# Gated attention and an MLP mixer on one core: the second channel product as seven block products in place of eight

## The chip, the cores and the metric

The kernel runs on one core of a Trainium2 chip. A core has five engines with a queue each, worked off in order: TensorE (PE, matmuls; its weight loads are listed apart as PEld), VectorE (DVE), ScalarE (ACT), GpSimd (POOL) and SyncE (SP, which here issues transfers). Sixteen DMA engines move data between the chip's memory (DRAM) and the core's on-chip memory, SBUF, and transpose blocks on the way. Matmul results land in PSUM. The metric is the time of one execution in microseconds (us), as a median of several runs.

## The reference

Inputs are `u`, `v` (8 batches × 3008 rows × 256), `z` (8 × 3008 × 64) and four mixer weights. All is float32; the kernel multiplies in bfloat16 and sums in float32.

```python
scores = (1.0 / S) * np.matmul(z, z.transpose(0, 2, 1))      # S = 3008
attn = np.maximum(scores, 0.0) ** 2
x = u * np.matmul(attn, v)

h = np.maximum(x.transpose(0, 2, 1) @ w_tok1, 0.0) @ w_tok2  # over the rows, 3008 -> 256 -> 3008
u1 = x + h.transpose(0, 2, 1)
h2 = np.maximum(u1 @ w_ch1, 0.0)                             # 256 -> 1536
out = u1 + h2 @ w_ch2                                        # 1536 -> 256
```

The last line's `h2 @ w_ch2` is the "second channel product", `u1 @ w_ch1` the first. They are called ch2 and ch1 below.

## The kernel before

**Tiles.** Rows are worked in query blocks of 512 (QW), six a batch (NQ), the last 448 wide; 448 is three tiles of 128 rows (P) and a half tile of 64, and the half tiles of an even batch and the next odd one are multiplied together ("hs", "ut"). The 1536 channels are 12 tiles of 128 (CHT).

**Stages.** For a batch, attention runs block by block: scores (L428), relu on ACT (L466), square on DVE (L474), the product with `v` (L657). The score matrix is symmetric, so a computed block also serves mirrored, by a DMA transpose on SP into a tile of the pool "fl" ("flip"). The copy and the add of the accumulators (L783, L789) and the gate with `u` (L810) give `x` with its columns on the partitions (pool "xT"); one more DMA transpose gives its rows (`turn_x`, pool "x"). Mixer: token product 1 (`tok1`, L864), token product 2 (`tok2`, L883) with its add into xT (L892), then for each query block six pieces of ch1 and up to four of ch2. Blocks 3 to 5 of one batch are mixed together with the token products and blocks 0 to 2 of the next, in one stretch of TensorE work of some 70 us before that batch's successor begins its attention. Seven such stretches follow a first short one.

**A piece of ch1** (`ch1`, L913): two channel tiles, eight matmuls at most 512 columns wide into a pair of PSUM banks (hp, L924), then one relu of the whole pair into a tile of the pool "h2", on ACT (L967) or on DVE (L969), whichever is expected to be free earlier (L960). **A piece of ch2** (`ch2`, L978): for one tile of 128 rows twelve matmuls, each with 128×128 of h2 as the loaded weights and 256 columns of `w_ch2` as the moving side (L993). Two pieces fill a bank; then one DVE add (L1009, or L1027 for the odd ends) puts `u1` to it in a buffer "res" (three of them), and SP sends this to the output (L1014, L1030). The rows of `u1` come by a DMA transpose on SP (`turn_u2`, L906, pool "us").

**The order.** It is fixed when the program is built. A planner goes through time with assumed costs: `Piece` is a piece of TensorE work with its needs, `push` puts work on ACT, DVE or SP, `run_engines` lets those queues come up to a time, `next_piece` (L1083) takes the next mixer piece out of two lists, `heads` (token products) and `tails` (ch1 and ch2). A piece that `opens` a PSUM pair is one of a chain until the one that `closes` it, and only one such chain is open at a time. `ROOM` (L316) limits the buffers of each pool that the plan has in use. PSUM has a ring of bank pairs. What the planner does not count still holds: the instructions wait, by semaphores, for the tiles, banks and buffers that they use. The tails of a batch are listed thus, with `early` being 2:

```python
        for q in range(NQ):
            for c2 in range(early if q else 0, CHT // 2):
                add_ch1(q, c2, q)
            if q + 1 < NQ:
                for c2 in range(early):
                    add_ch1(q + 1, c2, q)
            for half in halves(q):
                for i in range(pieces_of(q, half)):
                    add_ch2(q, half, i)
```

So all four pieces of ch2 of a block stand together, behind two pieces of ch1 of the next block.

Of the kernel before, what the change touches and what calls it, by code (L numbers as in the profile page):

```python
# [45 lines left out]
class Piece:  # L46


    def __init__(self, cost, needs, fn, opens=False, closes=False, room=None,
                 urgent=False, key=(0, 0)):  # L50
        self.cost, self.needs, self.fn = cost, needs, fn
        self.opens, self.closes, self.room = opens, closes, room
        self.urgent, self.key = urgent, key
# [3 lines left out]
def kernel(  # L57
# [42 lines left out]
    w_ch2_sb = consts.tile([P, CHT, D], BF16)  # L100
    ident = consts.tile([P, P], BF16)
# [53 lines left out]
    def first_z(c):  # L155

        zf = sb.tile([P, GK, d_qk], F32, tag="x", name="zf", bufs=7)
# [9 lines left out]
    def double_first_z(c):  # L167
        zr = sb.tile([P, GK, 2, d_qk], BF16, tag="h2", name="zr0", bufs=8)
        nc.vector.tensor_copy(zr[:], zf0[c].unsqueeze(2).to_broadcast([P, GK, 2, d_qk]))  # L169
        return zr  # L170
# [28 lines left out]
    def load_v(b, c):  # L199
# [5 lines left out]
        else:  # L205
            vt = sb.tile([P, GK, D], BF16, tag="v", name="v_sb", bufs=8)
# [108 lines left out]
    live = {"at": 0, "fl": 0, "xT": 0, "x": 0, "h2": 0, "us": 0}  # L315
    ROOM = {"at": 6, "fl": 10, "xT": 9, "x": 7, "h2": 8, "us": 2}  # L316
# [155 lines left out]
    def square(unit, view, t):  # L472
# [15 lines left out]
        if flips(b, q, g):  # L488
# [4 lines left out]
                        room=lambda: has_room(("fl",)) and (  # L493
# [21 lines left out]
    def flip_tiles(a3, j):  # L515
# [4 lines left out]
        return a3  # L520

# [93 lines left out]
    def do_whole(start, g):  # L615
# [19 lines left out]
        if final:  # L635
# [3 lines left out]
                room=("xT", "x") if dh == 0 else lambda: (blk.b, blk.q) in xTs)  # L639
# [127 lines left out]
    def finish(blk, dh, end):  # L767
# [12 lines left out]
        def copy(t):  # L780
            cp = sb.tile([P, QW], F32, tag="res", name="cp", bufs=3)
# [6 lines left out]
        def add(cp, t):  # L788
            nc.vector.tensor_add(cp[:, :W], acc[:, 0, :W], cp[:, :W])  # L789
            push("dve", t, 0.58, 0.7, lambda t: gate(blk, dh, cp, t), first=1,  # L790
                 room=(lambda: (blk.b, blk.q) in uTs and has_room(("xT", "x"))) if dh == 0
# [7 lines left out]
    def gate(blk, dh, acc, t):  # L799
        b, q, W = blk.b, blk.q, blk.W  # L800
        uT = uTs[b, q]
        if dh == 0:
            xTs[b, q] = sb.tile([P, DT, QW], BF16, tag="xT", name="xT", bufs=ROOM["xT"])
            live["xT"] += 1
            live["x"] += 1
# [11 lines left out]
        if dh == DT - 1:  # L817
            gated[0] += 1
            push("sp", t, 1.25, 7.5 if q < NQ - 1 else 12.0, lambda t: turn_x(b, q, t), first=1,
                 room=lambda: b == 0 or mode[0] == "full")  # L820

    def turn_x(b, q, t):
        x = sb.tile([P, DT, QW // P, P], BF16, tag="x", name="x_sb", bufs=ROOM["x"])
# [14 lines left out]
    before = [None]  # L838

# [7 lines left out]
    def add_mixer(b):  # L847
# [3 lines left out]
        h2_done = {}  # L851
# [60 lines left out]
        def ch1(q, c2, end):  # L912
# [3 lines left out]
            if c2 == 0:  # L916
                live["us"] += 1
                st["turned", q] = push("sp", u_done[q].t, 1.25, 5.5, lambda t: turn_u2(q))
            live["h2"] += 1
# [8 lines left out]
            def load(e):  # L928
                return max(free[e], end) + sum(op.busy for op in waiting[e])

# [7 lines left out]
            if (b, q, c2) == (B - 1, NQ - 1, CHT // 2 - 1):  # L938
                landed, freed = [], Done()

                def evacuate_part(r, t):
                    if not landed:
                        st["h2", q, c2] = sb.tile(
                            [P, 2, QW], BF16, tag="h2", name="h2pre", bufs=ROOM["h2"])
                    h2 = st["h2", q, c2]
# [14 lines left out]
            on_act = load("act") + 0.92 < load("dve") + 1.15  # L960

            def evacuate(t):
                h2 = sb.tile([P, 2, QW], BF16, tag="h2", name="h2pre", bufs=ROOM["h2"])
                st["h2", q, c2] = h2
# [5 lines left out]
                if q == NQ - 1:  # L970
                    keep_ends(h2)
            engine, busy = ("act", 0.92) if on_act else ("dve", 1.15)
            ring.append((push(engine, end + 0.21, busy, busy + 0.16, evacuate,
                              done=h2_done[q, c2]), slot))
            if c2 == CHT // 2 - 1:
                release("xT", xT_uses[q])

        def ch2(q, half, i, end):  # L978
# [9 lines left out]
            for cc in range(CHT):  # L988
                if both:
                    h2 = pair["hs"][:, cc, :]  # L990
                else:
                    h2 = st["h2", q, cc // 2][:, cc % 2, c0:c0 + P]
# [3 lines left out]
            over = i == pieces_of(q, half) - 1 and half == halves(q)[1]  # L996
            if over:
                live["h2"] -= CHT // 2
# [3 lines left out]
            def residual(t):  # L1002
                us = st["u", q]
                if q == NQ - 1 and b % 2 == 0 and half == 0:
                    pair["ut"] = sb.tile([TAIL, DT, P], BF16, tag="ut", name="ut", bufs=1)
                    nc.gpsimd.tensor_copy(pair["ut"][:], us[:TAIL, :, full_tiles[q], :])
                res = sb.tile([P, 2, D], F32, tag="res", name="res", bufs=3)
# [9 lines left out]
                else:  # L1017
                    k = half * 2
                    j = i if apart else 0
                    ends = [(j, slice(0, P), us[:, :, k + j, :],  # L1020
                             rows_of(out[b], q)[:, k + j, :])]
# [10 lines left out]
                if over:  # L1032
                    live["us"] -= 1
# [9 lines left out]
        def add_ch1(q, c2, by):  # L1043
            h2_done[q, c2] = Done()
            tails.append(Piece(4 * column_time(widths[q]), [u_done[q]] + w_done[:2],
                               lambda end: ch1(q, c2, end),
                               room=("h2", "us") if c2 == 0 else ("h2",),
                               key=(b, 2 + by)))

# [8 lines left out]
        def alone(q, half):  # L1058

            return pieces_of(q, half) == 1 or (b, q, half) == (B - 1, NQ - 1, 0)  # L1060

        def add_ch2(q, half, i):
            two = not alone(q, half)
            needs = [Sooner(h2_done[q, c2], 0.218 * c2) for c2 in range(CHT // 2)]
            tails.append(Piece(1.312, needs + w_done[2:],
                               lambda end: ch2(q, half, i, end), opens=two and i == 0,
                               closes=two and i == 1, key=(b, 2 + q)))


        early = ROOM["h2"] - CHT // 2  # L1070
        for q in range(NQ):
            for c2 in range(early if q else 0, CHT // 2):
                add_ch1(q, c2, q)
            if q + 1 < NQ:
                for c2 in range(early):
                    add_ch1(q + 1, c2, q)
            for half in halves(q):
                for i in range(pieces_of(q, half)):
                    add_ch2(q, half, i)
# [3 lines left out]
    def next_piece(t):  # L1083
# [3 lines left out]
        if opened[0] is not None:  # L1087
# [374 lines left out]
```

## Time and profile before

| what | value |
|---|---|
| runs, median (lowest to highest) | 1142.33 us (1141.83 to 1142.89) |
| span of the profiled execution | 1140.2 us |
| ch2 matmuls (L993) | 2208, 273 ns each as recorded |
| ch1 matmuls (L924) | 1152, 375 ns each |
| product with `v` (L657) | 2738 + 1680, 374 and 367 ns each |
| relu of ch1 on ACT (L967) / DVE (L969) | 159 of 998 ns / 128 of 1215 ns |
| granted TensorE clock | 9 tenths or more in all 40 slices |

The span is the profiler's, from the first to the last instruction; it is 2.1 us below the median of the runs. A recorded matmul lasts longer than the step from one to the next, since matmuls are pipelined; how long a stretch of them takes is read from the chain of waits or from the timeline. The idle time of an engine is given with its releaser, the instruction that ended it.

### The profile page before, as it was taken

The page shows a single profiled execution, that of the slowest core. Times are in us where ns is not written, and L with a number is a line of the kernel's source. Part 1 is how long each engine was busy: PE and PEld are TensorE (multiplying, and loading weights), DVE is VectorE, ACT ScalarE, POOL GpSimd, SP SyncE. Part 2 cuts the span into 40 slices and gives each one's busy share as a digit, 9 for nine tenths or more (in the row PEclk, how much of TensorE's full clock was granted, in tenths as well). Part 3 has the DMA queues.
Part 4 walks back from the last instruction along what each step waited for, and adds up shares of the span by engine and source line. Part 5 has one row for each costly group of instructions (what it writes and reads, how often), then busy time and mean ns, then how long its engine had stood idle before and what let it go on. Part 6 is the DMA issues. An engine that isn't in the chain of part 4 may idle for free.

```text
span 1140.2 us, 22490 instructions
## 1 busy us (share of the span) xinstructions
PE 1133.2 (99%) x9219; PEld 678.5 (60%) x9219; DVE 642.1 (56%) x953; ACT 549.3 (48%) x702; POOL 146.3 (13%) x387
## 2 busy tenths in 40 slices
PE   9999999999999999999999999999999999999998
PEld 3455464665557655576555765556655576556666
DVE  6887744464654556645565455654566544644543
ACT  7998635234752346522574236632366322732231
POOL 4500110221002110021101211012100120000000
PEclk9999999999999999999999999999999999999999
DMA  9999953987959878697986968679598794782122
GB/s 165 186 171 213 164 126 80 173 164 130 170 119 195 154 136 161 116 199 141 161 147 118 211 139 154 136 132 209 116 168 146 144 197 103 142 139 72 51 84 65
DMA packets 469928, 165.25 MB, mean 145 GB/s; under 512 B 433665, under 2 KB 447553, under 8 KB 469825
## 3 DMA queue, kind: packets, MB, share of 16 engines
q1 hardware_dynamic: 441968, 131.11, 56.7%
q0 software_dynamic: 27344, 32.32, 20.5%
q8 instruction: 72, 1.18, 0.4%
q10 hardware_dynamic: 512, 0.38, 0.1%
q14 instruction: 32, 0.25, 0.1%
HBM read 65.40 MB, written 24.64 MB: 79 GB/s over the span
## 4 chain that ended last, share of the span: by engine, by line
PE 98%; DMA 1%; DVE 0%; ACT 0%; issue 0%
PE acc L657 41%; PE op L993 22%; PE hp L924 21%; PE sc L428 6%; PE a_ps L864 4%; PE h_ps L883 3%; PE first_acc L573 1%; DMA zT<-zr 1%; DMA zf<-in_z_dram 0%; DVE zr L169 0%; ACT h2pre L967 0%; DVE h2pre L949 0%; ACT h2pre L947 0%; PE up L1257 0%; DVE res L1027 0%
## 5 line engine op out<-in xcount | busy, mean ns | idle before, releaser
L657 PEld LDWEIGHTS <-v_sb 64*128 64x128 bf16 x4418 | 241.9, 94 | 215.8 <-issue 1.8
L657 PE MATMUL acc<-at,v_sb 64*128 64x512 bf16 (+1 forms) x2738 | 338.8, 374 | 0.0
L466 ACT ACTIVATE at<-sc 128x1024 bf16<-128x1024 f32 (+1 forms) x290 | 286.2, 1026 | 73.4 <-PE sc L428 63.3
L967 ACT ACTIVATE h2pre<-hp 128x1024 bf16<-128x1024 f32 (+1 forms) x159 | 158.8, 998 | 310.8 <-PE hp L924 310.8
L474 DVE TENSOR_TENSOR at<-at 128x1024 bf16<-128x1024 bf16 (+1 forms) x290 | 197.5, 687 | 125.0 <-ACT at L466 120.9
L924 PE MATMUL hp<-xT,w_ch_sb 128*128 128x512 bf16 (+1 forms) x1152 | 255.3, 375 | 0.1
L993 PE MATMUL op<-w_ch_sb,h2pre 128*128 128x256 bf16 x2208 | 251.3, 273 | 0.1
L993 PEld LDWEIGHTS <-h2pre 128*128 128x128 bf16 x2208 | 216.0, 98 | 36.3 <-ACT h2pre L947 0.4
L969 DVE TENSOR_SCALAR h2pre<-hp 128x1024 bf16<-128x1024 f32 (+1 forms) x128 | 155.5, 1215 | 80.9 <-PE hp L924 80.9
L657 PE MATMUL acc<-fl,v_sb 64*128 64x512 bf16 (+1 forms) x1680 | 190.7, 367 | 0.0
L924 PEld LDWEIGHTS <-w_ch_sb 128*128 128x128 bf16 x1152 | 112.2, 98 | 126.7 <-issue 3.0
L1009 DVE TENSOR_TENSOR res<-op,u_sb 128x512 f32<-128x512 f32 x87 | 60.2, 691 | 174.9 <-PE op L993 170.9
L428 PE MATMUL sc<-zT 64*128 64x512 bf16 (+1 forms) x732 | 132.4, 359 | 0.6 <-DMA zT<-zr 0.5
L454 ACT ACTIVATE at<-sc 128x512 bf16<-128x512 f32 (+3 forms) x152 | 56.5, 442 | 84.0 <-PE sc L428 73.5
L789 DVE TENSOR_TENSOR cp<-acc,cp 128x512 f32<-128x512 f32 (+1 forms) x94 | 63.5, 675 | 38.2 <-ACT cp L783 37.8
L783 ACT COPY cp<-acc 128x512 f32<-128x512 f32 (+1 forms) x89 | 51.8, 582 | 54.8 <-PE acc L657 54.7
L506 DVE TENSOR_TENSOR at<-at 128x512 bf16<-128x512 bf16 (+3 forms) x152 | 42.1, 321 | 47.5 <-ACT at L454 47.5
L428 PEld LDWEIGHTS <-zT 64*128 64x128 bf16 x732 | 42.6, 94 | 43.4 <-issue 3.5
L810 DVE TENSOR_TENSOR xT<-cp,uT 128x512 bf16<-128x512 f32 (+1 forms) x94 | 62.4, 664 | 1.5
L892 DVE TENSOR_TENSOR xT<-xT,h_ps 128x1024 bf16<-128x1024 bf16 (+1 forms) x48 | 56.1, 1175 | 12.5 <-PE h_ps L883 12.4
L121 POOL CAST mark<-at 128x1 f32<-128x1 bf16 x12 | 2.3, 188 | 414.5 <-DVE at L474 414.5
L883 PE MATMUL h_ps<-w_tok_sb,a_sb 128*128 128x512 bf16 (+1 forms) x192 | 47.9, 375 | 0.0
(59 smaller groups left out, 315.0 us busy)
## 6 DMA issues: line engine op xcount, KB each, us to landing
out_dram<-res SPq DMA_DIRECT2D x87, 256.0 KB, 2.5
v_sb<-in_v_dram POOLq DMA_DIRECT2D x40, 256.0 KB, 5.7
ur<-in_u_dram POOLq DMA_DIRECT2D x40, 256.0 KB, 4.7
w_tok_sb<-in_moe_w_tok_dram POOLq DMA_DIRECT2D x10, 256.0 KB, 9.5
zs<-in_z_dram POOLq DMA_DIRECT2D x35, 64.0 KB, 2.8
at<-at SPq DMA_TRANSPOSE x114, 2.3
fl<-at SPq DMA_TRANSPOSE x105, 5.3
v_sb<-in_v_dram POOLq DMA_DIRECT2D x8, 192.0 KB, 5.0
```

The costliest lines, as they stand in the source:

```text
L428: nc.tensor.matmul(sc[:, r, c0:c1], zT[h, k:k + P], zT[h, m + c0:m + c1], start=True, stop=True)
L466: nc.scalar.activation(view, sv, ACT.Relu, scale=inv_S)
L474: nc.vector.tensor_mul(view, view, view)
L657: nc.tensor.matmul(o, vs[blk.b, g][rows, i, dh * P:(dh + 1) * P], rhs, start=(dh, h) not in blk.begun, stop=stop, skip_group_check=True)
L789: nc.vector.tensor_add(cp[:, :W], acc[:, 0, :W], cp[:, :W])
L810: nc.vector.tensor_mul(xT[:, dh, :full * P].rearrange("p (t s) -> p t s", s=P), acc[:, :full * P].rearrange("p (t s) -> p t s", s=P), uT[: ...
L883: nc.tensor.matmul(h[:, dh, :W], st["a"][:, th, dh * P:(dh + 1) * P], w_tok2_sb[:, th, q * QW:q * QW + W], start=(th == 0), stop=(th == 1))
L924: nc.tensor.matmul(hp[:, r, :W], w_ch1_sb[:, dc, cc * P:(cc + 1) * P], xT[:, dc, :W], start=(dc == 0), stop=(dc == DT - 1))
L967: nc.scalar.activation(h2[:, :, :W], hp[:, :, :W], ACT.Relu)
L969: nc.vector.tensor_single_scalar(h2[:, :, :W], hp[:, :, :W], 0.0, AX.max)
L993: nc.tensor.matmul(op[:, i, :], h2, w_ch2_sb[:, cc, :], start=(cc == 0 and (i == 0 or apart)), stop=(cc == CHT - 1), skip_group_check=True)
L1009: nc.vector.tensor_add(res.rearrange("p i (h d) -> p i h d", d=P), op.rearrange("p i (h d) -> p i h d", d=P), us[:, :, half * 2:half * 2 + ...
```

## The change

The second channel product of a query block is computed by Winograd's form of Strassen's scheme. Let A be a block of h2 of two row halves by two channel tiles, and B the two channel tiles by two column halves (128 each) of `w_ch2`. A·B, with 2×2 blocks, takes eight block products. The scheme makes four sums of blocks of A (s1 to s4) and four of B, seven block products, and result adds that collect them. Here TensorE sums a product over all six pairs of channel tiles in PSUM, and products 1, 6, 7, 4 follow one another in the same bank half, so that each result add reads a running sum.

- Each of the seven is a `Piece` of its own (`product`): 6 × J matmuls of 128 columns. J is 2 (256 rows), and 1 for the 448-wide block, whose other rows stay with the old `ch2`. Block 5 of the last batch and blocks 0 to 2 of the first stay with it wholly (`fast`).
- The sums of h2 are four DVE operations for each four channel tiles (`add_sums`), those of `w_ch2` four more, once (`sum_weights`).
- Six DVE adds collect the result (`adds`), and two output transfers of 256 KB at J = 2 leave after the third and the fourth.
- The pool "h2" is gone. h2 (four channel tiles to a buffer) and the sums are in "fl", which has 14 buffers in place of 10; the pool "x" has 6 in place of 7. `flips_fit` limits how many of them mirrored blocks may hold.
- Products lie in the list between the ch1 pieces of the next block; two chains may be open at a time (`n_open`). The groups of a batch are blocks 0 to 2 and 3 to 5, in the last batch all six.
- The choice between ACT and DVE for a relu counts 0.85 us for the sums (`SUMS_TO_COME`).

```diff
-    live = {"at": 0, "fl": 0, "xT": 0, "x": 0, "h2": 0, "us": 0}
-    ROOM = {"at": 6, "fl": 10, "xT": 9, "x": 7, "h2": 8, "us": 2}
+    RES = 3
+    live = {"at": 0, "fl": 0, "xT": 0, "x": 0, "us": 0, "mix": 0, "res": 0}
+    ROOM = {"at": 6, "fl": 14, "xT": 9, "x": 6, "us": 2, "res": RES}
+    MIRRORS = 10
+    U_TURN = 0
+    SUMS_TO_COME = 0.85
+    AHEAD = 2
...
+    def flips_fit(b):
+
+        n = live["fl"] - live["mix"]
+        return n < (MIRRORS if b < 2 else AHEAD if in_mixer[0] else ROOM["fl"])
...
-            on_act = load("act") + 0.92 < load("dve") + 1.15
+            on_act = load("act") + 0.92 < load("dve") + 1.15 + SUMS_TO_COME * fast(q)
...
+        def fast(q):
+
+            return (b > 0 or q >= NQ // 2) and (b, q) != (B - 1, NQ - 1)
+
+        def columns(q):
+            return P if q == NQ - 1 else 2 * P
+
+        def add_sums(q, c4, t):
...
+            a11, a12 = h[:, :, 0, :n], h[:, :, 1, :n]
+            a21, a22 = h[:, :, 0, n:2 * n], h[:, :, 1, n:2 * n]
...
+            def s1(t):
+                nc.vector.tensor_add(new()[0], a21, a22)
+
+            def s2(t):
+                nc.vector.tensor_sub(new()[1], new()[0], a11)
+
+            def s3(t):
+                nc.vector.tensor_sub(new()[2], a11, a21)
+
+            def s4(t):
+                nc.vector.tensor_sub(new()[3], a12, new()[1])
...
+        def product(q, m, end):
...
+            f = st["f", q].rearrange("p r (h j d) -> p r h j d", h=2, d=P)
+            part = {1: f[:, 0, 0], 6: f[:, 0, 0], 7: f[:, 0, 0], 4: f[:, 0, 0],
+                    2: f[:, 0, 1], 5: f[:, 1, 0], 3: f[:, 1, 0]}[m]
+            for c2 in range(CHT // 2):
+                h2, k = st["h2", q, c2 // 2], c2 % 2
+                if m in (1, 2, 4):
+                    lhs = {1: h2[:, 2 * k, :n], 2: h2[:, 2 * k + 1, :n],
+                           4: h2[:, 2 * k + 1, n:2 * n]}[m]
+                else:
+                    lhs = st["s", q, c2 // 2][:, {5: 0, 6: 1, 7: 2, 3: 3}[m], k, :n]
+                if m in (1, 2, 3):
+                    rhs = {1: w_ch2_sb[:, 2 * c2, :P], 2: w_ch2_sb[:, 2 * c2 + 1, :P],
+                           3: w_ch2_sb[:, 2 * c2 + 1, P:]}[m]
+                else:
+                    rhs = w_sums[:, {5: 0, 6: 1, 7: 2, 4: 3}[m], c2, :]
+                for j in range(J):
+                    nc.tensor.matmul(
+                        part[:, j, :], lhs[:, j * P:(j + 1) * P], rhs,
+                        start=m in (1, 5) and c2 == 0 and j == 0, stop=c2 == CHT // 2 - 1,
+                        skip_group_check=True)
...
+        def adds(q, m, end, f, J):
+
+            us = st["u", q]
+            a, b_, n = f[:, 0, 0, :J], f[:, 1, 0, :J], full_tiles[q]
...
+            def first(t):
+                nc.vector.tensor_add(res(0)[:, :, 0], a, us[:, 0, :J])
+
+            def fifth(t):
+                nc.vector.tensor_add(res(1)[:, :, 1], b_, us[:, 1, J:2 * J])
+
+            def sixth(t):
+                nc.vector.tensor_add(res(0)[:, :, 1], a, us[:, 1, :J])
+
+            def seventh(t):
+                nc.vector.tensor_add(res(1)[:, :, 1], a, res(1)[:, :, 1])
+
+            def third(t):
+                o = res(0).rearrange("p t h d -> p h t d")
+                both = f.rearrange("p r h j d -> p (r h) j d")[:, 1:3, :J]
+                nc.vector.tensor_add(o, both, o)
+                put(0)
+
+            def fourth(t):
+                nc.vector.tensor_add(res(1)[:, :, 0], a, us[:, 0, J:2 * J])
+                put(1)
...
+                m = p[q]
+                out_pieces += e[:2] + [m[1]]
+                if q + 1 == group[-1] and fast(q + 1):
+                    n = p[q + 1]
+                    out_pieces += [e[2], m[5], e[3], e[4], m[6], e[5], m[2], m[3],
+                                   n[1], m[7], n[5], n[6], m[4]]
+                    out_pieces += d[q + 1][:1] + [n[2], n[7]] + d[q + 1][1:] + [n[3], n[4]]
+                    if q + 1 == NQ - 1:
+                        closing.extend([n[7], n[4]])
+                else:
+                    out_pieces += [m[5], e[2], m[6], e[3], m[2], e[4], m[7], e[5], m[3], m[4]]
+            tails.extend(out_pieces)
...
+    def sum_weights(t):
+        w = w_ch2_sb.rearrange("p (k r) (h d) -> p k r h d", r=2, d=P)
+        b11, b12, b21, b22 = w[:, :, 0, 0], w[:, :, 0, 1], w[:, :, 1, 0], w[:, :, 1, 1]
+        nc.vector.tensor_sub(w_sums[:, 0], b12, b11)
+        nc.vector.tensor_sub(w_sums[:, 2], b22, b12)
+        nc.vector.tensor_add(w_sums[:, 1], w_sums[:, 2], b11)
+        nc.vector.tensor_sub(w_sums[:, 3], b21, w_sums[:, 1])
```

In the list, `c` and `e` are ch1 pieces of a block and of the next, `m` and `n` the products of these two, and `d` the old pieces that a 448-wide block keeps. The two pieces in `closing` are put before which the first ch1 pieces of the next group come.

## The prediction

> **What bounds the kernel now.** I read the page first, then the chain of waits, the windows, the groups by form, and the timeline at three places.
>
> ```profile
> span 1140.2 us, 22490 instructions
> PE 1133.2 (99%) x9219; PEld 678.5 (60%) x9219; DVE 642.1 (56%) x953; ACT 549.3 (48%) x702; POOL 146.3 (13%) x387
> PE 98%; DMA 1%; DVE 0%; ACT 0%; issue 0%
> out_dram<-res SPq DMA_DIRECT2D x87, 256.0 KB, 2.5
> ```
>
> The page: TensorE (PE) is the bound, with no idle time to win back; only shorter matmul work can pay, and any new PE wait costs in full. An output DMA lands 2.5 us after issue.
>
> ```profile
> 339.20:411.50 72.30, 72.30 (x507) 49.24 (x506) 36.54 (x41) 21.07 (x22) 15.22 (x42) 1.00 0.88 159
> 479.40:550.40 71.00, 71.00 (x496) 48.07 (x496) 35.77 (x39) 21.07 (x22) 15.85 (x44) 1.00 0.88 160
> ```
>
> Windows over two mixer stages (us; busy PE, PEld, DVE, ACT, POOL; granted clock; DMA share; GB/s): PE is full, the clock 1.00; VectorE (DVE) is busy half of it.
>
> ```profile
> 142.11 5.24 PE op L993 x48
> ```
> ```profile
> L993 PE MATMUL op<-w_ch_sb,h2pre 128*128 128x256 bf16 x2208 | 251.3, 273 | 0.1
> L1009 DVE TENSOR_TENSOR res<-op,u_sb 128x512 f32<-128x512 f32 x87 | 60.2, 691 | 174.9 <-PE op L993 170.9 <-DMA out_dram<-res 4.0
> L506 DVE TENSOR_TENSOR at<-at 128x512 bf16<-128x512 bf16 x38 | 16.0, 422 | 47.5 <-ACT at L454 47.5
> L1027 DVE TENSOR_TENSOR res<-op,u_sb 128x256 f32<-128x256 f32 x10 | 4.2, 424 | 9.1 <-issue 5.2 <-PE op L993 3.8
> ```
> ```profile
> 21.50 0.65 PEld L1257 LDWEIGHTS <-ur 128*128 128x128 bf16 x8
> 21.71 0.61 PE L1257 MATMUL up<-ident,ur 128*128 128x128 bf16 x8
> ```
> ```profile
> L1257 PE MATMUL up<-ident,ur x8: 219/219/219, 21.7 to 22.1; 128*128 128x128 bf16 x8
> ```
>
> The chain gives ch2's price: 5.24/48 = 0.1092 us a step of 256 columns, weight load included. The set-up's eight 128-column matmuls, each with its own load (98 ns alone), give the products' price: (0.61 − 0.219)/7 = 0.0559 us. So a load hides.
>
> ```profile
> 1095.41 0.27 PE L993 MATMUL op<-w_ch_sb,h2pre 128*128 128x256 bf16 x1
> 1095.72 0.69 DVE L1009 TENSOR_TENSOR res<-op,u_sb 128x512 f32<-128x512 f32 x1 [1.93 <-PE op L993]
> 1096.44 0.33 SPq L1014 DMA_DIRECT2D out_dram<-res  x1
> ```
> ```profile
> 1130.45 0.54 ACT L947 ACTIVATE h2pre<-hp 128x448 bf16<-128x448 f32 x1 [0.44 <-DVE h2pre L949]
> 1131.05 0.10 PEld L993 LDWEIGHTS <-h2pre 128*128 128x128 bf16 x1 [0.37 <-ACT h2pre L947]
> ```
>
> The timeline gives the hand-overs. The last matmul's row ends at 1095.68 and runs 0.164 (0.273 − 0.109) past its step; DVE starts at 1095.72: 0.20 from PE's step to DVE. DVE ends 1096.41, the DMA issues at 1096.44: 0.03. A reader ends at 1130.99, PE loads at 1131.05: 0.06.
>
> **The saving.** The built order has 1944 fewer L993 matmuls and 3402 products of 128 columns; ch1, token and attention matmuls keep their counts. 1944 × 0.1092 = 212.3 us off, 3402 × 0.0559 = 190.1 us on: **22.2 us** saved, and 0.2 more at the end, where the wait at 1131.05 gets products 3 and 4 of the block before it as cover: 22.4. In the 448-wide blocks (J=1) a product's six matmuls, 294 in all, add into the same 128 columns each time, where the eight wrote different ones. Bounds: nothing, or L993's step, which also adds into one place, 294 × 0.053 = 15.7 us; I take nothing, since L993's 0.109 is no more than twice 0.056, its columns.
>
> One page speaks against it: the Trainium skill, "TensorE: Matmul & The Clock Gate", on the back-to-back issue gap, has a sustained load-and-matmul stream at N=128 spaced about 81 ns. By it, an estimate, the products would take 275.6 us and the kernel would lose 63 us instead of saving 22. The row above shows 55.9 ns, but over only eight.
>
> **Vector work.** Relus leave DVE (128 become 9; ACT has 159 → 279), 87 L1009 adds become 6. Added: 444 sums of 512 bf16 and 84 of 256 (0.40 by L506's rows); 37 × (5 adds of 256 f32 and one of 512 = 2.8); 7 × six smaller (12 in all). 642 − 119 × 1.22 + 528 × 0.40 − 81 × 0.69 + 37 × 2.8 + 12 = 768 us, 19 us more in a stage: 36 + 19 = 55 of 71. ACT: 549 + 120 × 1.02 = 671. Hidden under PE, at nothing but the waits below; it costs where an add is late. In a full queue the next op starts early:
>
> ```profile
> 128.28 0.69 DVE L789 TENSOR_TENSOR cp<-acc,cp 128x512 f32<-128x512 f32 x1
> 128.89 0.42 DVE L506 TENSOR_TENSOR at<-at 128x256 bf16<-128x256 bf16 x2
> ```
>
> 0.08 before the end, so a 0.42 op steps by 0.34. The four weight sums (768 wide, some 2.2 us) run once, behind batch 0's attention; uncovered, they cost 2.2. SP issues 112 output DMAs for 105, and the same transposes. The "h2" tiles move into "fl" (10 → 14 buffers), and mirrored blocks are held to 2 while the mixer takes tiles, so attention may open a stage with fewer turned; by the built order each stretch keeps its scores and values. I take nothing; the bound is one late transposed tile (fl<-at lands in 5.3 us) a stage, 7 × 5.3 = 37.
>
> **The waits.** This is what decides. One pair of banks f holds a block's seven products: 1, 6, 7, 4 in one half bank, 2 beside it, 5, 3 in the other. In the built order a product waits for the last read of *any* part of f, and a read for the last product queued before it in f. And "res" has three buffers: the second open block's add5 waits until the first's output, sent after add3, has landed (L). Both chains are short where ch1's 0.87 us pieces lie between; they bite where none are left. Below, m is the last block but one of a group and n the last; m7 is m's seventh product, add7 its result add.
>
> *Stage end* (6 times; order m3, n1, m7, n5, n6, m4, n2, n7, n3, n4; a product 12 × 0.0559 = 0.67). From m3's end: add3 starts at 0.20, ends 0.89, so m7 starts at 0.95, not 0.67: 0.28. m4 would end at 0.95 + 4 × 0.67 = 3.63. The output leaves at 0.92, lands at 0.92 + L; then add5n 0.34, a sum 0.34, add6n 0.42, with two hand-overs 0.11: n2 at 2.13 + L. L: near the stage ends the landings' medians are 2.6, 2.0, 3.1, 2.2, 2.6, 2.2, mean 2.4:
>
> ```profile
> DMA to landing us min/median/max: 2.0/2.0/2.2
> ```
> ```profile
> DMA to landing us min/median/max: 2.1/3.1/3.2
> ```
>
> (Source view of L1014, windows 396 to 412 and 535 to 551.) n2 at 4.53: 0.90. add7n is queued behind n3's record, so n4 waits 0.20 + 0.42 + 0.06 = 0.68 after it. Sum 1.86, × 6 = **11.2 us** (L = 2.0: 8.8; L = 3.8: 20). The DVE's sums and SP's next transposes wait behind add5n and nobody on PE for them.
>
> *Seam between block 4 and block 5 in a stage*: here m3, tok2, n1, m7, n5, tok2 take 0.87 + 0.34 + 0.67 + 0.34 + 0.87 = 3.09; n6 needs add5n, at 0.92 + L + 0.05 + 0.29 + 0.06 (0.29: the 256 row less half a slope, (0.691 − 0.424)/256 × 128). Whole-stage landing medians are 3.1, 3.0, 3.6, 3.0, 3.7, 2.9, so L = 3.2: 1.4; with tok2's and n4's waits 0.45: about 1.9, 4 times (even batches). In odd batches (3 times) a ch2 piece waits for a u′ add (0.35), the next for a residual behind a landing (0.3), n4 for add3 behind two such residuals (1.4): about 2.1. Sum 7.6 + 6.3 = **13.9** (L = 2.5: 8; 3.8: 22).
>
> *Group start*: m6 waits for add5, which is behind add1: 0.20 + 0.34 + 0.42 + 0.06 = 1.02 against ch1's 0.87: 0.15 for 7 groups; in 7 others a sum stands between: 0.49; batch 7's inner blocks 1.7: 1.1 + 3.4 + 1.7 = **6.2** (bounds 0, if DVE is ahead, and 7 × 1).
>
> Middle blocks (m and next ch1 in turn) show no wait in such a walk up to L = 4.2. Sum: 11.2 + 13.9 + 6.2 = 31.3. Span 1140.2 − 22.4 + 31.3 = 1149.1. The median of the runs stands 2.1 above that profiled span, so **1151 us**. Bounds: L = 2.0 everywhere and group starts half, 8.8 + 4 + 3 = 16, gives 1136; L = 3.8, 20 + 22 + 7 = 49, gives 1169.
>
> **Rivals.** (1) *Saving comes through* (other side): the adds are early, landings near 2.0, the planner's order leaves PE other pieces: stalls under 3.2 us a stage (22.4/7) turn it. For: DVE is 44% idle. Against: the order on PE is fixed, and the named waits have no piece to put in between. With no stalls at all 1119.9; with half, 1135. Chance 0.20.
> (2) *Level*: the stalls come to 20 to 25 us: 1142. Chance 0.12.
> (3) *Matmuls of 128 columns bound by the load*: at L1257's 98 ns each instead of 55.9, 3402 × 0.042 = 143 us more: 1263 without stalls. Against: the eight rows. Chance 0.03.
> (4) *DVE becomes the bound*: if sums ran at the f32 row's 0.69 instead of 0.42, 528 × 0.27 = 142 us, 20 us a stage: 75 against 70, so about +35 over the forecast, 1185. Against: the L506 row, same type and width. Chance 0.04.
> That the change doesn't do what it says is excluded by the counts.
> (5) the forecast, stalls of 25 to 50 us: 1145 to 1169. Chance 0.61.
>
> **Numbers.** Changes under 0.2% (2.3 us) can't be told from none here. Faster: rival 1, 0.20. Same 0.12. Slower 0.61 + 0.03 + 0.04 = 0.68. The range takes the forecast's own, 1145 to 1169, which holds the J=1 bound too (1167), and goes down to half the stalls, 1136; left out are rival 1's lower part (0.1), 3 and 4 (0.07), and a transposed tile late in every stage (1188).
>
> **What would show it.** Right: products in steps of 56 ns; PE idle some 30 us, before a product, released by DVE adds, and DVE's add5 idle on out_dram; 4 to 5 us in each stage. Wrong: PE busy 99% (rival 1), products at 81 to 98 ns (3), DVE over 95% in a stage (4), or landings well below 2 us or above 4.

## The result, and the profile after

| | before | after |
|---|---|---|
| median of the runs | 1142.24 us (1141.83 to 1142.89, 4 runs) | 1183.11 us (1180.65 to 1187.32, 4 runs) |
| ratio | | 1.0349, 95% interval 1.031 to 1.0389 |
| span of the profiled execution | 1140.2 us | 1182.7 us |

The kernel is 3.5% slower. The page of the changed kernel:

```profile
span 1182.7 us, 26007 instructions
PE 1128.1 (95%) x10603; PEld 684.0 (58%) x10677; DVE 734.0 (62%) x1547; ACT 659.1 (56%) x823; POOL 153.2 (13%) x387
PE 74%; DMA 13%; DVE 5%; ACT 4%; SPq 2%; issue 2%; ACTq 0%; DVEq 0%
```

TensorE's share of the chain of waits fell from 98% to 74%; transfers took 13% of it. So the kernel is no longer bound by TensorE alone, though TensorE is still busy 95% of the time.

The trace splits by what TensorE works on: the mixer stretches (ch1, ch2, products, token products) and the attention stretches between them. Each is measured here from its first matmul to the first of the next stretch.

| stretch | before, us | after, us | difference |
|---|---|---|---|
| first, short mixer stretch | 38.58 | 37.31 | −1.3 |
| mixer, even batches (three) | 70.99 each | 75.10, 77.76, 78.94 | +18.8 |
| mixer, odd batches (three) | 72.30 each | 73.86, 74.16, 75.29 | +6.4 |
| last mixer stretch | 100.22 | 100.45 | +0.2 |
| attention, five in the middle | 67.88 each | 73.07, 71.44, 71.86, 69.48, 72.85 | +19.3 |
| attention, last | 65.45 | 65.45 | 0 |

The sum is +43.5 before rounding; the opening took 0.5 more and the tail after the last matmul 1.5 less, which leaves the +42.5 of the spans. Nearly half of the loss lies in attention, where the change adds no TensorE instruction.

The view of what TensorE waited for, over the whole span (us in total, times, longest):

```profile
PE f L1080 <- DVE res L1124: 14.5, 18, 3.4
PE f L1080 <- DVE res L1127: 8.8, 6, 2.6
PE sc L435 <- ACT at L473: 3.7, 6, 0.8
PE f L1080 <- DVE res L1130: 3.1, 6, 0.5
PE acc L671 <- DMA at<-at: 3.0, 5, 1.1
PE f L1080 <- DVE res L1135: 2.6, 4, 1.6
```

L1080 is the products; L1124 is add5, L1127 add6, L1130 add7, L1135 add3. The `sc` and `acc` lines are attention. In the kernel before, this view held 1.7 us, all of it in the set-up. The views count a wait from the end of the last matmul's record; TensorE's waits named in the text are counted from that matmul's step, which ends some 0.16 us earlier, so 3.29 in a view is 3.45 in the text.

What add5 in turn waited for (source view of L1124):

```profile
  DMA out_dram<-res: 23.9, 10
  PE f L1080: 8.3, 7
```

Ten waits for the landing of an output transfer, 23.9 us. One of them in the timeline, at a seam (between blocks 4 and 5 of a batch):

```profile
523.37 8.50 SPq L1115 DMA_DIRECT2D out_dram<-res  x2
...
523.64 1.17 PE L1080 MATMUL f<-w_sums,sums 128*128 128x128 bf16 x18
...
528.62 0.29 DVE L1124 TENSOR_TENSOR res<-f,u_sb 128x128 f32<-128x128 f32 x1 [3.15 <-DMA out_dram<-res]
...
528.97 0.80 PE L1080 MATMUL f<-w_sums,sums 128*128 128x128 bf16 x6 [3.29 <-DVE res L1124]
```

The transfer issued at 523.37 frees its buffer only at 528.6; add5 waits for the buffer, and product 6 for add5. The second line also gives the products' price: (1.17 − 0.221)/17 = 0.0558 us from one matmul to the next.

The clock: four times in the stages TensorE ran at half speed for 3.41 us, from 269.6, 529.0, 822.5 and 860.1 us of the span. Each time this began within 0.4 us of the end of a long wait: waits of 2.46, 3.45, 3.59 and 2.44 us ended at 269.66, 528.97, 822.17 and 860.30. In the windows view (length; busy time and count of each engine; granted clock, DMA share, GB/s) of one even stage, the attention behind it, and the seam alone:

```profile
493.06:570.82 77.76, 69.94 (x684) 49.25 (x692) 47.92 (x119) 35.73 (x38) 16.07 (x42) 0.98 0.77 137
570.82:642.68 71.86, 69.08 (x651) 35.90 (x649) 41.70 (x78) 43.93 (x65) 3.09 (x9) 1.00 0.77 152
525.00:530.00 5.00, 1.71 (x15) 1.23 (x13) 1.85 (x5) 0.00 (x0) 0.00 (x0) 0.90 0.56 108
```

The same attention stretch in the kernel before:

```profile
550.37:618.25 67.88, 67.88 (x650) 35.91 (x649) 40.53 (x77) 43.83 (x65) 2.45 (x7) 1.00 0.80 146
```

The stage has 7.8 us without TensorE work, its attention 2.8; VectorE is busy 47.9 of 77.8, so it is not the bound.

What stands behind the attention rows is seen on SyncE. The timeline of its queue at the start of the same attention stretch, before (from 271.3) and after (from 274.7):

```profile
272.64 2.75 SPq L138 DMA_TRANSPOSE zT<-zs  x2
275.44 1.23 SPq L142 DMA_TRANSPOSE zT<-zs  x1
276.76 3.77 SPq L518 DMA_TRANSPOSE at<-at  x3
```

```profile
276.42 6.07 SPq L540 DMA_TRANSPOSE fl<-at  x1
282.66 3.33 SPq L140 DMA_TRANSPOSE zT<-zs  x2
286.03 1.23 SPq L144 DMA_TRANSPOSE zT<-zs  x1
287.36 1.63 SPq L540 DMA_TRANSPOSE fl<-at  x1
289.09 4.95 SPq L525 DMA_TRANSPOSE at<-at  x3
```

A mirrored block's transpose now stands ahead. The next batch's z comes 1.3 us into the stretch before and 8.0 us after; the first transposes of a block on the diagonal (`at<-at`) come after 5.4 and 14.4 us. Counted over the whole of this stretch, SyncE is occupied with issuing for 58.7 of 67.9 us before and for 68.0 of 73.1 after: two of the five mirrored transposes that ran inside the mixer have moved into attention (10 became 12).

How this reaches TensorE is seen in what ScalarE waited for. A relu of the scores writes a tile of the pool "at", and that tile is free only when the mirrored transpose that read its last content has landed. Before (L454, L466) and after (L461, L473), over the whole span:

```profile
ACT at L454 <- DMA fl<-at: 9.9, 2, 5.0
ACT at L466 <- DMA fl<-at: 5.8, 4, 1.9
```

```profile
ACT at L473 <- DMA fl<-at: 33.0, 24, 4.6
ACT at L461 <- DMA fl<-at: 13.1, 8, 3.9
```

So 15.7 us became 46.1, all of it in the five middle attention stretches. Before, TensorE had no wait in these stretches; after, its view above has the `sc` lines, score products that wait for a relu, and the `acc` lines.

### The profile page after: what moved, and what is told of

Read it like the earlier page. It is cut to its first block, busy times and chain, and to the rows that moved or that the text cites. A ratio compares the mean times of both kernels' runs of the same rounds, so it can differ in the third digit from the quotient of the medians.

```text
span 1182.7 us, 26007 instructions
## 1 busy us (share of the span) xinstructions
PE 1128.1 (95%) x10603; PEld 684.0 (58%) x10677; DVE 734.0 (62%) x1547; ACT 659.1 (56%) x823; POOL 153.2 (13%) x387
## 4 chain that ended last, share of the span: by engine, by line
PE 74%; DMA 13%; DVE 5%; ACT 4%; SPq 2%; issue 2%; ACTq 0%; DVEq 0%
PE acc L671 29%; PE hp L950 17%; PE f L1080 15%; DMA fl<-at 7%; PE sc L435 5%; PE a_ps L887 4%; DMA out_dram<-res 3%; PE op L1175 3%; PE h_ps L906 2%; ACT at L473 2%; DMA u_sb<-xT 2%; SPq L525 1%; ACT h2pre L1003 1%; DVE res L1124 1%; PE first_acc L587 1%
## 5 line engine op out<-in xcount | busy, mean ns | idle before, releaser
L1003 ACT ACTIVATE h2pre<-hp 128x1024 bf16<-128x1024 f32 (+1 forms) x279 | 269.2, 1014 | 242.2 <-PE hp L950 216.1
L473 ACT ACTIVATE at<-sc 128x1024 bf16<-128x1024 f32 (+1 forms) x290 | 284.6, 1024 | 87.2 <-PE sc L435 50.3
L950 PE MATMUL hp<-xT,w_ch_sb 128*128 128x512 bf16 (+1 forms) x1095 | 265.3, 375 | 2.1
L671 PE MATMUL acc<-fl,v_sb 64*128 64x512 bf16 (+1 forms) x1680 | 195.6, 368 | 2.8 <-ACT at L473 1.9
L950 PEld LDWEIGHTS <-w_ch_sb 128*128 128x128 bf16 x1152 | 106.6, 98 | 98.0 <-issue 2.9
L1080 PEld LDWEIGHTS <-sums 128*128 128x128 bf16 x1944 | 121.7, 99 | 40.9 <-issue 21.8
L1080 PE MATMUL f<-w_sums,sums 128*128 128x128 bf16 x1458 | 101.9, 221 | 15.4 <-DVE res L1124 14.5
L1080 PEld LDWEIGHTS <-h2pre 128*128 128x128 bf16 x1458 | 92.8, 99 | 34.9 <-issue 18.3
L461 ACT ACTIVATE at<-sc 128x512 bf16<-128x512 f32 (+3 forms) x152 | 55.1, 445 | 98.0 <-PE sc L435 84.3
L1039 DVE TENSOR_TENSOR sums<-h2pre 128x512 bf16<-128x512 bf16 (+1 forms) x132 | 53.6, 406 | 70.0 <-ACT h2pre L1003 69.9
L1080 PE MATMUL f<-w_ch_sb,h2pre 128*128 128x128 bf16 x972 | 69.9, 222 | 8.9 <-DVE res L1127 8.8
L915 DVE TENSOR_TENSOR xT<-xT,h_ps 128x1024 bf16<-128x1024 bf16 (+1 forms) x48 | 55.5, 1169 | 3.9 <-PE h_ps L906 3.8
```

Of the source, the lines that this page charges most:

```text
L461: nc.scalar.activation(a3[:, i, c0:c1], sc[:, r, c0:c1], ACT.Relu, scale=inv_S)
L473: nc.scalar.activation(view, sv, ACT.Relu, scale=inv_S)
L671: nc.tensor.matmul(o, vs[blk.b, g][rows, i, dh * P:(dh + 1) * P], rhs, start=(dh, h) not in blk.begun, stop=stop, skip_group_check=True)
L915: nc.vector.tensor_add(to, to, h[:, :, :n * P].rearrange("p h (s t) -> p h t s", t=n))
L950: nc.tensor.matmul(hp[:, r, :W], w_ch1_sb[:, dc, cc * P:(cc + 1) * P], xT[:, dc, :W], start=(dc == 0), stop=(dc == DT - 1))
L1003: nc.scalar.activation(h2[:, :, :W], hp[:, :, :W], ACT.Relu)
```

## The experiments

Every ratio is against the kernel before on the same chip, with its 95% interval.

| experiment | ratio to before | profiled span, us |
|---|---|---|
| four result buffers | 1.0124 (1.0061 to 1.0187) | 1157.0 |
| before, mirrored blocks held | 1.0095 (1.0059 to 1.0131) | 1152.1 |
| last block of a group plain | 1.0074 (1.0039 to 1.0110) | 1151.5 |
| no sums | 1.0334 (1.0269 to 1.0398) | 1186.8 |
| no sums, four result buffers | 0.9964 (0.9944 to 0.9983) | 1137.8 |
| last plain, more room for transposes | 1.0043 (1.0015 to 1.0071) | 1150.6 |
| the same, another order of products | 1.0142 (1.0099 to 1.0184) | 1147.7 |
| more room, u in another pool | 0.9934 (0.9894 to 0.9974) | 1133.3 |
| its control with eight products | 1.0040 (1.0000 to 1.0081) | 1157.8 |
| more room, three u buffers | 0.9993 (0.9965 to 1.0021) | 1139.4 |

### A fourth result buffer

```diff
-    RES = 3
+    RES, RES_BUFS = 3, 4
...
-            cp = sb.tile([P, QW], F32, tag="res", name="cp", bufs=RES)
+            cp = sb.tile([P, QW], F32, tag="res", name="cp", bufs=RES_BUFS)
...
-                    st["a"] = sb.tile([P, 2, D], BF16, tag="a", name="a_sb", bufs=1)
+                    st["a"] = sb.tile([P, 2, D], BF16, tag="x", name="a_sb", bufs=ROOM["x"])
```

(The same for the two other `res` tiles; the plan still counts three. The last edit makes the space.)

> One part of the change's waits taken away: a fourth result buffer for the output transfers, with every queue's order unchanged. My theory: the long waits of products 6 and 2 of the last block of a group are for the landing of an output transfer (2.46, 0.73, 2.73, 0.73, 2.44, 0.68 us at the six stage ends; 1.19, 3.45, 3.59 us and smaller ones at the seams). They go, some 19 us with the 3.4 us of lowered clock that follow them in the mixer, so about 1162 to 1165 us; the attention stretches stay at 69 to 73 us. Rival (the adds are late because VectorE is full, the transfer only happens to end then): the waits move to another releaser and the time stays within 4 us of 1183. Second rival (waits behind the landing were also shelter for the next wait in the chain): half comes back, 1173.

Measured 1161.5 us. No wait for a landing is left in the view of add5's waits. Below it are the stage of 77.76 us and the attention behind it in the windows view:

```profile
  PE f L1080: 15.9, 16
```

```profile
486.60:557.46 70.86, 69.21 (x693) 48.24 (x692) 47.74 (x119) 35.74 (x38) 16.18 (x42) 1.00 0.80 141
557.46:628.98 71.52, 69.09 (x650) 35.87 (x649) 41.67 (x78) 43.97 (x65) 3.11 (x9) 1.00 0.83 159
```

The stage of 77.76 us takes 70.86, the granted clock is 1.00 throughout, and attention is nearly as long as before this edit (71.52; the five middle stretches together 2.1 us shorter). The mixer stretches together come to 0.4 us above those of the kernel before: what is saved in matmuls is then spent on the remaining waits of 0.13 to 0.8 us, some 23 us in all. The landing theory holds, and the lowered clock went with the waits.

### The kernel before, with its mirrored blocks held

```diff
-                        room=lambda: has_room(("fl",)) and (
+                        room=lambda: has_room(("fl",)) and flips_fit(b) and (
...
+    in_mixer = [False]
+
+    def flips_fit(b):
+        return b < 2 or not in_mixer[0] or live["fl"] < 2
...
+        in_mixer[0] = any(p.takes and p.key <= goal[0] for p in tails)
```

> The kernel before with one part of the change alone: while mixer pieces that take tiles are left, no more than two mirrored blocks are held, so that three of their transposes a stage move from the middle of the mixer to its end and to the attention after it. No product and no sum. My theory (attention pays because SyncE's queue is full there): the five middle attention stretches go from 67.9 us to 70 to 73, the mixer stages stay at 71.0 and 72.3, the total is 1155 to 1162 us. Rival (attention loses time through the later relus on ScalarE, the sums or the lowered clock, and the place of the transposes costs nothing): 1142 to 1144 us.

Measured 1157.1 us, ratio 1.0095. Mixer stages 70.99 and 72.30 as ever; the middle attention stretches 69.36, 68.82, 71.84, 68.23 and 72.63 us, 11.5 in all, which is the whole difference of the spans (1152.1 − 1140.2 = 11.9). No product, no sum, no changed relu is in this kernel. One of these stretches, and ScalarE's waits over the span:

```profile
553.35:625.19 71.84, 68.59 (x650) 35.88 (x649) 40.31 (x77) 43.12 (x65) 2.46 (x7) 1.00 0.77 156
```

```profile
ACT at L467 <- DMA fl<-at: 34.1, 13, 4.7
ACT at L455 <- DMA fl<-at: 10.4, 3, 5.4
```

The number of mirrored transposes hardly moves (4 or 5 in a stage instead of 5, 10 or 11 in attention instead of 10); what moves is their place. Before, all five of a stage are issued in its first 31 us; here two are, and the others from 64 us on. This alone costs 11.5 us, against the 19.3 in the changed kernel, where two have moved into attention altogether.

### The last block of a group without products

```diff
-            return (b > 0 or q >= NQ // 2) and (b, q) != (B - 1, NQ - 1)
+            return (b > 0 or q >= NQ // 2) and q not in (NQ // 2 - 1, NQ - 1)
```

> The change without seven products for the last block of each group (blocks 2 and 5), which takes the eight of before. Gives up some 5 us of the matmul saving. My theory: the waits at stage ends and seams (some 36 of 45 us in the mixer) go, the group starts (0.48 and 0.15 us) stay; mixer stages near 69 to 71 us; the attention stretches keep most of their loss, since transposes still stand at the end of the mixer: 1145 to 1155 us. Rival (the waits are not of the group ends but of the scheme, and move to the block that is now last with products): 1170 to 1180 us.

Measured 1153.9 us. Mixer stages of 69.8 (one of 70.5) and 71.1 us, 1.2 below the kernel before; attention 71.8, 67.9, 73.5, 73.4, 72.7. So the scheme as such pays, in the blocks that have ch1 of the next one to lie between, and the attention loss is apart from it (ScalarE waits 53.6 us for mirrored transposes).

### No sums

```diff
-                if fast(q) and len(sides[q, c2 // 2]) == 2:
-                    add_sums(q, c2 // 2, max(sides[q, c2 // 2]))
+                return
...
-                    lhs = st["s", q, c2 // 2][:, {5: 0, 6: 1, 7: 2, 3: 3}[m], k, :n]
+                    lhs = h2[:, 2 * k, :n]
...
-    AHEAD = 2
+    AHEAD = 8
```

(The sums take no buffers either, and up to eight mirrored blocks may be held in place of two. So VectorE's load and the room for transposes change together here; the kernel with more room, below, keeps the sums of all blocks that have products.)

> The sums of h2 are left out, so the products multiply the blocks of h2 themselves and the output is not the reference's. Same products, same result adds and transfers; VectorE has 212 us less to do, half of the mixer's tiles are free and four mirrored blocks are turned in the middle of the mixer again. My theory: the attention stretches are back at 68 us (19 us less), the waits for landing transfers stay near 25 to 30 us of 45, since VectorE was not what they waited for: 1155 to 1163 us. Rival (VectorE's load makes the adds late): the mixer's waits fall under 10 us, 1130 to 1140 us. Second rival (attention's loss has nothing to do with tiles): attention stays at 70 to 73 us.

Attention came as expected: 67.88 us in all five. The mixer did not: stages of 77.7 to 81.2 us, the total 1185.4. The window of one stage and of the attention after it, and a seam:

```profile
493.90:574.84 80.94, 72.88 (x692) 50.76 (x691) 22.95 (x47) 35.64 (x38) 15.12 (x42) 0.94 0.72 134
574.84:642.72 67.88, 67.88 (x650) 35.74 (x649) 40.78 (x78) 43.74 (x65) 3.10 (x9) 1.00 0.85 153
```

```profile
375.48 7.89 SPq L540 DMA_TRANSPOSE fl<-at  x2
383.46 4.94 SPq L1114 DMA_DIRECT2D out_dram<-res  x2
```

```profile
386.09 0.29 DVE L1123 TENSOR_TENSOR res<-f,u_sb 128x128 f32<-128x128 f32 x1 [5.89 <-DMA out_dram<-res]
```

With VectorE busy for only 23 of 81 us the waits got longer, so its load is not the cause. The output transfer, ready after add3 at 377.4, is issued only at 383.5, behind the mirrored transposes that now run in the mixer; add5 waits 5.9 us, and behind it in VectorE's queue stand the adds into xT for which token product 2 and ch2 wait. The two shortages hang together: transposes in the mixer delay the outputs that three buffers wait for, transposes held back delay attention.

### No sums, and a fourth result buffer

The edits of both.

> The kernel without sums (its output is not the reference's; the sums of h2 are left out), with a fourth result buffer, every queue's order unchanged. Without that buffer its result adds waited 45.5 us for landing transfers, which on SyncE stood behind the transposes now back in the middle of the mixer. My theory: with both shortages gone, buffers for results and tiles for transposes, the saving is there: attention 67.9 us, mixer stages 69.5 to 71 and 70.5 to 72.5 us, total 1132 to 1142 us. Rival (the transposes and the output transfers also delay the token rows or the u blocks on the same queue): stages stay over 74 us, 1160 us or more.

Measured 1139.7 us, ratio 0.9964: mixer stages 70.1, 72.2, 71.2, 72.7, 71.2, 73.4, attention 67.9 (68.3 once). By the two ratios some 42 us fell away with one buffer. The two shortages account for nearly all of the loss, but not for a gain of 22: waits of 0.28, 0.34 and 0.68 us at each stage end and 0.3 to 2.0 at the seams remain, some 21 us in all, and they eat most of the 2.9 us that a stage saves.

### More room for transposes

```diff
-        ur = sb.tile([P, QW // P, D], BF16, tag="ur", name="ur", bufs=3)
+        ur = sb.tile([P, QW // P, D], BF16, tag="ur", name="ur", bufs=2)
...
-    ROOM = {"at": 6, "fl": 14, "xT": 9, "x": 6, "us": 2, "res": RES}
+    ROOM = {"at": 6, "fl": 15, "xT": 9, "x": 6, "us": 2, "res": RES}
...
-    AHEAD = 2
+    AHEAD = 3
...
+        if b >= 2 and 0 < in_mixer[0] <= 3:
+            return live["fl"] + in_mixer[0] < ROOM["fl"]
```

(With the last block plain; the token tile in the x pool as above. `in_mixer` counts the tiles still to be taken.)

> The kernel without products for the last block of a group, and with room for transposes in the mixer: a fifteenth buffer in the shared pool (paid by one of three u buffers and by laying the small token tile into the x pool), three mirrored blocks held in place of two, and more as soon as only the last block's tiles are still to be taken. Per stage one or two transposes fewer stand at the mixer's end. My theory (attention pays for transposes that stand ahead of its own on SyncE): the stretches that took 71.8 to 73.5 us fall to 68 to 69.5, the mixer stages stay within 0.5 us of 69.8 to 71.1: 1133 to 1142 us, 0.99 to 1.00 of before. Rival (the attention loss comes of the mixer's vector work or of the lowered clock after waits): the stretches stay at 71 to 73 us, 1150 to 1154 us. Rival on the price paid (one u buffer less makes gates late): attention as before or longer, with waits for u.

Attention 67.92, 67.88, 67.92, 68.10 and 69.57 us, mixer stages 69.81 and 71.12: as my theory had it. ScalarE's waits for mirrored transposes are down to 5.2 us. The total was not as expected, 1151.2 us (1137.9 to 1157.2): in the profiled run, of 1152.3 us, the opening stretch took 116.6 us instead of 99.4. GpSimd, which issues the loads, waited there 30.9 us (19.9 at the longest) for a u buffer to be transposed, against 10.1 in the kernel before, and TensorE 12.6 us for z, which is loaded by the same queue.

```profile
POOL ur L222 <- DMA uT<-ur: 30.9, 3, 19.9
PE sc L435 <- DMA zT<-zs: 12.6, 2, 8.7
```

### Another order of a block's products

```diff
-                    out_pieces += [m[5], e[2], m[6], e[3], m[2], e[4], m[7], e[5], m[3], m[4]]
+                    out_pieces += [e[2], m[5], m[2], m[6], e[3], m[7], e[4], m[3], e[5], m[4]]
```

(On the kernel above; the same order where the next block has no products.)

> As the kernel with more room for transposes, and the products of a block laid so that a piece of ch1 or another product stands between each one and the reader of the last: 1, ch1, 5, 2, 6, ch1, 7, ch1, 3, ch1, 4. My theory: the waits of 0.14 at each group start and 0.5 before product 4 go, 0.6 to 1 us a stage, 5 us in all: 1128 to 1137 us. Rival (they were shelter for the next ch1 pieces' relus, which now are waited for): the same within 2 us as without the new order.

A miss: the mixer stages rose from 69.81 and 71.12 to 71.78 and 72.5, with waits of 0.68 us. (The median of the runs was 1163.2 us, the profiled run took 1149.7; what made others longer than that isn't in its trace.) Seen in its timeline:

```profile
212.46 0.83 PE L1082 MATMUL f<-w_ch_sb,h2pre 128*128 128x128 bf16 x12
213.33 0.42 DVE L1126 TENSOR_TENSOR res<-f,u_sb 128x256 f32<-128x256 f32 x1 [0.50 <-PE f L1082]
```

The first line is product 2, the second add5. Product 5 had ended 0.67 us earlier, in the other bank of the pair, but the read waits for product 2, the last one queued into the pair, and product 6 then waits for the read. A product of the same pair in between gave no cover here: 0.68 us is the whole of the read, where the order with ch1, on another pair, had left at most 0.54.

### The u blocks of the opening in an empty pool, and its control

```diff
-        ur = sb.tile([P, QW // P, D], BF16, tag="ur", name="ur", bufs=2)
+        ur = sb.tile([P, QW // P, D], BF16, tag="us" if b == 0 and q % 2 else "ur", name="ur", bufs=2)
```

> The kernel with more room for transposes (products for all blocks but the last of a group), every queue's order unchanged, but the first batch's odd u blocks are loaded into the pool us, which is empty then, so that the opening has its buffers for u again. My theory: the opening stretch, 116.6 us there, is back at 99.4; the middle attention stretches stay at 67.9 to 69.6 and the mixer stages at 69.8 and 71.1, 1.2 us under those of the kernel before: 1131 to 1135 us, 0.990 to 0.994 of before. Rival (the opening lost for another reason than u's buffers): 1149 to 1152 us.

Measured 1137.2 us, ratio 0.9934: 0.7% faster than the kernel before. Opening 100.5, attention 67.9 to 68.6, mixer stages 69.81 and 71.12. Its stage and attention in the windows view:

```profile
477.92:547.73 69.81, 68.86 (x628) 48.02 (x638) 38.85 (x87) 35.58 (x38) 16.07 (x43) 1.00 0.88 157
547.73:615.93 68.20, 68.10 (x650) 37.53 (x649) 40.68 (x77) 43.73 (x65) 3.17 (x9) 1.00 0.84 147
```

In the control `fast` returns `False` for every block.

> The same with eight block products everywhere, no sums: the control for the seven. My theory: the seven save 0.54 us a block less their waits, 1.2 us a stage, so this one is 6 to 10 us slower than its neighbour: mixer stages 71.0 and 72.3, 1139 to 1145 us. Rival (the neighbour's gain is the layout's, not the products'): within 2 us of the neighbour.

```profile
493.74:565.21 71.47, 70.85 (x489) 47.96 (x494) 35.68 (x39) 21.14 (x22) 16.34 (x45) 1.00 0.90 156
```

The control's stages are 71.46 and 72.77 us, 1.65 longer than with seven products, so the gain of a stage is the products'. They are also 0.47 longer than those of the kernel before, so against that kernel 1.18 us a stage is left. The control's total, 1150.5 us, is 13 longer and not 6 to 10: in the traces its mixer stretches take 12.3 us more (1.65 in each of six, 2.4 in the last). Its opening took 113.0 us besides, in a profiled run of 1159.6 us, with waits for z. With fewer u buffers, or with another pool for them, the opening's length varied from one profiled run to the next (100.5, 103.4, 113.0, 116.6 us); why the same buffers gave 100.5 in one kernel and 113.0 in the other stays open.

### Three u buffers, eight xT buffers

```diff
-    ROOM = {"at": 6, "fl": 15, "xT": 9, "x": 6, "us": 2, "res": RES}
+    ROOM = {"at": 6, "fl": 15, "xT": 8, "x": 6, "us": 2, "res": RES}
```

(`ur` with its three buffers again.)

> Products for all blocks but the last of a group, a fifteenth buffer for transposes, with the three u buffers of the change kept and eight instead of nine xT buffers paid for it. My theory: the opening, 100.5 to 116.6 us with fewer u buffers or another pool for them, is at 99.4 in each run, so the runs lie closer together; attention 67.9 to 70, mixer 69.8 and 71.1: 1131 to 1137 us. Rival (the opening's length does not come of u's buffers): it stays between 103 and 117 us; or the missing xT buffer costs a wait for gates, over 1140 us.

Measured 1141.4 us, ratio 0.9993. The opening is 99.3 us, nine of ten runs lie within 3 us, attention is 67.9 throughout. But the plan is another with eight xT buffers: waits of 0.85 and 0.48 us before the first products of each stage, stages of 71.0 to 71.2 and 72.2 us. The gain is gone.

## Why the prediction was wrong

The direction held and the mechanism of the waits held; the size did not: 1151 with a range to 1169, measured 1183. By its own steps:

- **The saving.** 0.0559 us for a 128-column matmul was measured as 0.0558 over eighteen in a row; the median step of the products is 56 ns, in the J = 1 blocks too (six matmuls that repeat the same columns take 0.50 us at 536.61, (0.50 − 0.221)/5 = 0.0558). So the 81 ns that the Trainium skill gives in "TensorE: Matmul & The Clock Gate", on the back-to-back issue gap, for sustained pairs at N=128, is not what this kernel shows. The saving of 22.4 us is there, 2.9 us in a stage. Rivals 3 and 4 fall: loads hide, and the sums take 423 ns as L506's row had it. VectorE was busy for 734 us, 768 were worked out, and for 47.9 us in a stage where I had 55. The six matmuls, and one of the four kinds of sums:

```profile
536.61 0.50 PE L1080 MATMUL f<-w_sums,sums 128*128 128x128 bf16 x6
```

```profile
L1042 DVE TENSOR_TENSOR sums<-sums,h2pre 128x512 bf16<-128x512 bf16 x111 | 47.1, 424 | 3.4
```

- **The short waits** are as worked out: 0.28 for product 7 and 0.68 for product 4 at a stage end, each measured 0.28 (one 0.39) and 0.68; 0.48 for most second groups, worked out as 0.49.
- **The landing.** I took 2.4 us at stage ends and 3.2 at seams, from medians. In the odd stages that was right (0.68 to 0.73 us for product 2, 0.90 worked out; the seams 1.1, 2.0, 2.2 against 2.1). In the even ones the transfer landed in 4.2 us at one stage end, and took some 5.2 at a seam, while a load of u was in flight (that the load made it late was not tested); product 2 waited 2.4 to 2.7 us and product 6 up to 3.6. Together with the first products of a stage (up to 1.5 us, 0.15 worked out) the waits come to some 41 us instead of 31.3. The terms were right in kind, and the fourth buffer shows it; their size was taken from a median where the stage decided which side of it applied.

```profile
DMA to landing us min/median/max: 4.2/4.2/4.2
```

(Source view of the output transfer of the changed kernel, 562 to 564 us.)

- **The clock** was left out. With four of the long waits came 3.41 us at half speed each, a loss of at most 1.71, half of it, so up to 6.8 us. The sum of the mixer is then at most −22.4 + 41 + 6.8 = 25.4; measured are 24.2.
- **The step that failed most** is "I take nothing" for the mirrored blocks that are held to two while the mixer takes tiles. It was priced at 0 with a bound of 37 us, on the ground that each attention stretch keeps its scores and values. The number of matmuls is kept; what changed is what stands ahead of attention's transposes on SyncE, and with it when the tiles for the relus come free. It cost 19.3 us, inside the bound that the prediction named, but the range left that bound out. Holding the transposes in the kernel before reproduces 11.5 of these without anything else; with the tiles free (no sums) all 19.3 go; with the last block plain they were 19.8, and with more room for transposes besides and the sums of the other blocks kept, 2.0. The profile before had the warning: SyncE occupied for some 58 of 67.9 us in each attention stretch, against 38 to 47 of some 71.6 in a mixer stage, so the two transposes had little room where they went.

Forecast 1149.1 for the span, and what it missed: some 10 us of waits, up to 6.8 of clock, 19.3 of attention, and 1 less at the ends: about 1184, against the 1182.7 of the trace.

## What to carry to other kernels

When a change takes buffers from a pool, ask which transfers those buffers allowed to run early, and read the occupation of the queue in the stage where they will run instead; a count of matmuls per stage does not show it. A saving of 0.5 us a block is less than one exposed read of PSUM (0.68 us), so a chain of dependent products pays only where work on other banks lies between all its links, here in all blocks but the last of a group. And a buffer that is freed by a landing must be planned with the landing of its own stage and not with a median over many: here 3.9 to 4.2 us at the ends of the even stages, where 2.4 had been taken.

## What the runs showed of the hardware that was not expected

In the changed kernel TensorE dropped to half clock for 3.41 us at single waits of 2.44 to 3.59 us in a busy stretch, in four of the five cases (at one of 2.73 us it did not); without the long waits (a fourth buffer) the granted clock was 1.00. With waits of 4 to 7 us (no sums) it was halved for 3.4 to 10.2 us each time, and there it was halved for 3.41 us after three waits of some 2.2 us as well; the mean clock was 0.979. In the kernel with the last block plain it fell in attention, at 571.6 after waits of 2.4 and 0.7 us by the view, and at 714.9 after three of 0.4, 0.8 and 0.9 us that ended within 2.5 us. So the length of a single wait did not decide it.
